# A decode kernel whose instruction orders are written out: rearranged from token 1's first dense chain on

## The chip, the cores and the metric

The kernel runs on one core of one Trainium2 chip. Its time is that of one execution on the device, in microseconds (us). TensorE is called PE (its weight loads PEld), VectorE DVE, ScalarE ACT, GpSimd POOL, and SyncE SP; SP issues the loads.

## The reference

Four tokens, one position each, go twice through the same pair of layers: attention over a cache (the last 2048 of 8192 positions, 16 query heads on 8 key/value heads of width 256), then a gated feed-forward layer. Each is added to its input.

```python
W = min(4096, max(256, Sk // 4))                       # 2048
q = (x @ wq).reshape(B, Sq, Hq, Dh).transpose(0, 2, 1, 3)      # B 4, Sq 1, Hq 16, Dh 256
k = jnp.repeat(k_cache[:, :, Sk - W:, :], rep, axis=1)
v = jnp.repeat(v_cache[:, :, Sk - W:, :], rep, axis=1)
p = softmax(jnp.einsum("bhqd,bhkd->bhqk", q, k) * Dh ** -0.5)
o = jnp.einsum("bhqk,bhkd->bhqd", p, v)                # then transposed, reshaped, @ wo
...
g = silu(x @ w_gate); u = x @ w_up; return (g * u) @ w_down    # 448 -> 1792 -> 448
...
x = x + A(layernorm(x)); x = x + B(layernorm(x))
x = x + A(layernorm(x)); x = x + B(layernorm(x))
```

Both layers use the same weights and the same cache, so the keys and values that the second layer needs are those that the first has read, as far as they are still on the chip.

## The kernel before

A program on the host first builds a list of operations (`Graph.op`, L196; `Graph.dma`, L224), each with its engine and with what it reads and writes; from these follow the semaphore waits (`_place_waits`, L316). The order in which each engine runs its operations is not planned: it is written out as five lists of operation numbers, `SEQ_PE`, `SEQ_DVE`, `SEQ_ACT`, `SEQ_POOL` and `SEQ_SP`, near the top of the file. The number of an operation is its place in the order of building. `schedule` (L240) takes the lists as they stand. Each engine runs its list strictly in order, so an operation whose input is late holds up all behind it on its engine.

A `w` in `SEQ_PE` is a filler: one matmul of 512 columns by a weight of zeros into the bank A, which changes no result (L1253). `HELD` says, for each operation outside PE that touches bank A, behind how many fillers it comes.

K and V are loaded in halves of 512 KB into 31 slots and, once the query weights have been used for the last time, into the 7 places that these took (`SLOTS`; L976 and L978 for K, L992 for V). A load into a slot that is in use waits until the last PE operation that reads the old content is through; SP issues the loads in the order of `SEQ_SP`, and a load that waits holds up those behind it.

The unit of attention work is a group: two key/value heads of one token, or of two. `PLAN` says which. Its steps:

- L982: DVE transposes each half of K in place (four per group).
- L1023: POOL or DVE spreads the query (`qe`).
- L1016: PE, the scores, a block of 64 short matmuls or fewer (L1016 operations free K slots); L1031: DVE takes the maximum.
- L1036, L1039: PE spreads the maximum; L1045: DVE; L1049: ACT, the exponential.
- L1060: PE turns the probabilities; L1068: ACT copies; L1076, L1081: their sum; L1103: POOL, its reciprocal.
- L1090: PE, probabilities by V, in four parts (these free V slots); L1105, L1107, L1113, L1123: to the attention output.
- L1143 or L1135: PE, the output projection by `wo`, as a row or as a column.

When all groups of a token's layer are through, its dense chain follows, one token alone: the residual (L883 to L903), the norm (L589 to L629), gate and up (L801, 56 matmuls each in four operations, closed by L816), the activation (L832, L835), gate times up (L846), down (L853, four operations), the second norm, and the query projection of the next layer (L683 to L722). The first layer's chains of the tokens 1, 2 and 3 run near 125 to 145, 177 to 194 and 229 to 250 us of the profiled execution.

The numbers that the change moves and the prediction names:

| numbers | what | engine |
|---|---|---|
| 559 to 562, 564 to 567 | first chain: gate, up | PE |
| 572 to 575 | first chain: down | PE |
| 655, 660 | scores and turn of the probabilities of a group of token 0's second layer | PE |
| 627 to 630 | probabilities by V of a group of token 2 | PE |
| 888 to 891, 893 to 896 | second chain: gate, up | PE |
| 901 to 904 | second chain: down | PE |
| 947 | scores of token 3's first group | PE |
| 934, 936, 940, 942 | transposes of that group's K halves | DVE |
| 878 to 880 | second chain: the norm's sums | DVE |
| 1211, 1215, 1217 | transposes of K halves of token 1's second layer | DVE |
| 1091, 1126 | maxima of two groups of token 3 | DVE |
| 1163 to 1166, 1168 to 1171 | third chain: gate, up | PE |
| 1176 to 1179 | third chain: down | PE |
| 1174, 1175 | third chain: L835, L846 | DVE |
| 1231 to 1234 | probabilities by V of a group of token 1's second layer | PE |
| 1269, 1263, 1265 and 1276 | transposes and scores of a group of token 2's second layer | DVE, PE |

Of the kernel before, what the change touches and what calls it, by code (L numbers as in the profile page):

```python
# [62 lines left out]
    "49 w w w w w 53 w w w 56 w 64 w w w w 67 w 75 w 78 w 86 w 99 89 w 100 102 103 105 w w w 106 w 108 w w w w w 134 "  # L63
    "171 136 173 w w 139 204 141 176 w w 206 143 144 209 178 145 146 180 w 211 w w w w w w 213 214 215 216 150 245 "
    "155 156 247 w w 181 182 183 250 w w 252 187 254 255 256 257 220 w w 227 228 229 230 261 268 270 271 w w 275 w "
    "278 284 288 289 290 285 291 286 287 343 w w w 345 297 298 299 348 300 w 350 w 304 352 315 316 308 317 353 319 "
    "320 322 w w w 323 325 354 355 w 368 391 370 359 w w 393 362 363 373 414 396 375 398 400 401 402 377 378 403 379 "
    "380 416 384 419 w w 421 w w 407 w w w w w w w w w 387 388 423 424 425 426 w 410 411 w w w 451 453 w w w w w 486 "
    "456 430 w w 488 433 434 458 460 461 491 462 w 493 495 496 w w w w w w 521 463 497 498 523 467 w w 526 w w 528 "
    "470 w 502 618 471 530 505 620 506 531 532 533 623 542 w 625 w 537 544 545 w w w 559 560 561 548 627 628 552 562 "  # L70
    "w w w w w 564 565 566 567 655 563 568 657 w 572 573 574 660 575 w 662 w 579 590 591 583 592 664 594 595 597 629 "
    "630 598 w w 665 666 600 634 w w 637 638 697 720 699 w 722 741 667 702 w 743 w 704 w 671 725 706 707 708 727 709 "
    "746 674 675 729 748 730 731 732 750 751 752 678 713 753 w w w w 780 682 736 w w w 782 757 716 717 w 785 w 815 "
    "686 760 761 787 762 763 817 789 790 791 w 820 w 822 792 824 825 w w w 796 w w w w w 850 799 800 852 855 826 827 "
    "857 w w w 859 860 831 w w 834 835 861 862 871 866 w w w w w w 873 874 877 888 889 881 890 891 w w w 893 894 895 "
    "896 947 892 897 w 949 w 901 902 903 904 952 w 908 w 919 954 920 912 956 921 923 924 957 926 958 959 927 929 w "
    "963 w w 966 967 993 972 995 w w w w w 974 1018 977 w w w 998 979 w w 1000 1020 981 982 983 984 1002 1003 1004 "
    "1005 988 w w w w w w w 1009 w w 1023 w w 1053 1025 1012 1013 1014 1015 1055 w w w 1027 1028 1058 1029 1030 1060 "
    "w w w w w 1062 w 1034 w w 1125 w 1090 1127 w w w w 1092 1063 1222 1064 1095 w 1224 w 1097 1065 1130 1099 1100 "
    "1101 1069 1102 1132 1074 1075 1227 1072 1134 1106 1073 1229 w 1109 1110 1135 1136 1137 1146 w w w w 1141 w w "  # L80
    "1148 1149 1152 1163 1164 1156 1231 1165 1168 1169 1166 1167 1232 1233 1170 1171 1172 w w w w w w 1276 1176 1177 "
    "1278 1178 1179 w 1281 1183 1194 1234 1283 1187 1195 1198 1196 1199 1238 1285 1286 1201 1202 1241 1242 1287 1204 "
    "1299 1341 1245 1301 w w w w w 1304 1368 1343 1288 1306 1249 w 1370 1253 1308 1309 1292 1310 1311 1346 1403 1348 "
    "1315 1373 w 1405 1320 1318 1319 1321 1350 1351 1352 1353 1408 1375 1324 1377 1378 1410 1357 1328 1379 1380 1412 "
    "1413 1414 1415 1332 1362 1384 1364 1365 1387 1419 1388 1422 1423 1426 1441 1442 1430 1443 1444 1446 1447 1445 "
    "1448 1449 1450 w w w 1456 1457 1458 1459 w w 1461 w w w"
).split()
# [1242 lines left out]
```

## Time and profile before

| | |
|---|---|
| median of 3 runs | 279.63 us (278.82 to 279.69) |
| profiled execution | 279.5 us |
| its span | 277.7 us |
| mean granted clock of PE | 0.97 |
| PE busy | 209.0 us (75%) |
| DVE busy | 173.8 us (63%) |
| loads, mean over the span | 346 GB/s read |
| fillers (L1253) | 223 |

The span runs from the first to the last instruction of the program. Busy shares are means over stages with different limits, so the windows of single stages say more. PEclk is the share of PE's clock that was granted. "DMA" is the busy share of the core's DMA engines; at 1.00 and above, the stream of loads is full. A line with "issue" in the chain is time in which the engine waited for nothing that the profile shows. SPq is SP's queue, in which the loads are issued.

### The profile page before, as it was taken

Reading aid. Unit: us, or ns where it says so; the run is one execution under the profiler, and the core shown is the slowest. Engines: PE = TensorE matmul, PEld = TensorE weight load, DVE = VectorE, ACT = ScalarE, POOL = GpSimd, SP = SyncE. Lnnn points to the kernel's source line nnn. Section 1 sums busy time; section 2 is a strip of 40 time slices with the busy share of each in tenths; the row PEclk is TensorE's granted clock in tenths of the full one; section 3 lists DMA queues with packets and bytes.
Section 4 is the critical chain, followed back from the end, with each engine's and each line's share of the span. In section 5 each row is a group of like instructions: output and inputs, shape, how many; then the busy total and the mean of one; then the engine's idle time right before and its main releaser. Section 6 shows DMA issues by size and latency. Waiting matters only on the chain.

```text
span 277.7 us, 9966 instructions
## 1 busy us (share of the span) xinstructions
PE 209.0 (75%) x4424; PEld 125.0 (45%) x4424; DVE 173.8 (63%) x522; ACT 47.3 (17%) x115; POOL 76.5 (28%) x195
## 2 busy tenths in 40 slices
PE   0000076699788968988998897899699798899997
PEld 0000032355464634455754444474454356456694
DVE  7973056445545799368447995655789845559751
ACT  0000000232111220121113221211022031032510
POOL 1000017142204412421253342124132332043650
PEclk9999999999989999999999999999979999599998
DMA  7999999999999999999799999939999999589200
GB/s 292 394 419 412 403 412 406 402 396 401 389 379 405 357 396 415 407 409 353 260 332 410 409 405 411 405 150 362 362 417 407 410 408 346 215 279 408 79 5 1
DMA packets 28474, 96.68 MB, mean 348 GB/s; under 512 B 2828, under 2 KB 6928, under 8 KB 27792
## 3 DMA queue, kind: packets, MB, share of 16 engines
q1 hardware_dynamic: 28423, 96.06, 88.8%
q8 instruction: 34, 0.56, 0.8%
q14 instruction: 9, 0.07, 0.1%
q10 hardware_dynamic: 8, 0.00, 0.0%
HBM read 96.05 MB, written 0.00 MB: 346 GB/s over the span
## 4 chain that ended last, share of the span: by engine, by line
PE 43%; DMA 25%; DVE 13%; SPq 10%; issue 4%; ACT 3%; POOL 2%; ACTq 0%
DMA half<-in_A_k_cache_dram 16%; PE A L1253 10%; DMA half<-in_A_v_cache_dram 9%; PE S L1016 8%; DVE half L982 7%; PE Y L1090 6%; SPq L992 5%; PE Z L801 4%; SPq L976 3%; PE Z L683 3%; SPq L558 2%; PE Z L853 2%; PE A L1143 2%; PE Y L1060 2%; PE A L1135 2%
## 5 line engine op out<-in xcount | busy, mean ns | idle before, releaser
L982 DVE STREAM_TRANSPOSE half<-half 128x1024 uint32<-128x1024 uint32 x80 | 97.2, 1231 | 22.3 <-DMA half<-in_A_k_cache_dram 22.2
L1253 PE MATMUL A<-identb,small 128*128 128x512 bf16 x223 | 67.4, 404 | 0.3 <-DVE xr L903 0.3
L1103 POOL TENSOR_TENSOR small<-small 128x4 f32<-128x4 f32 x32 | 32.5, 1017 | 70.1 <-DVE small L1081 64.7
L1090 PE MATMUL Y<-half,pT 128*8 128x256 bf16 x1024 | 38.7, 275 | 3.2 <-issue 1.4
L1016 PE MATMUL S<-half,qe 128*8 128x256 bf16 (+1 forms) x1120 | 35.3, 269 | 6.3 <-issue 2.0
L1016 PEld LDWEIGHTS S<-half,qe 128*8 128x8 bf16 x1120 | 24.4, 84 | 16.2 <-issue 3.8
L1023 POOL TENSOR_TENSOR qe<-qc,small 128x64 bf16<-128x64 bf16 x56 | 15.3, 295 | 47.6 <-PE S L1016 33.9
L921 PE MATMUL Z<-identb,wo_sb 4*128 4x4 bf16 x4 | 0.3, 167 | 36.7 <-DMA wo_sb<-in_A_x_dram 36.7
L1031 DVE TENSOR_REDUCE small<-S 104x1 bf16<-104x256 f32 x32 | 13.4, 417 | 22.0 <-PE S L1016 22.0
L1090 PEld LDWEIGHTS Y<-half,pT 128*8 128x8 bf16 x1024 | 21.3, 85 | 12.0 <-DVE small L1081 3.2
L1253 PEld LDWEIGHTS A<-identb,small 128*128 128x128 bf16 x223 | 19.1, 103 | 14.9 <-issue 6.4
L1105 ACT ACTIVATE oh<-Y 128x256 bf16<-128x256 f32 x32 | 12.2, 383 | 36.2 <-PE Y L1090 27.2
L615 POOL TENSOR_SCALAR st<-st 128x1 f32<-128x1 f32 x16 | 4.5, 280 | 50.1 <-DVE st L609 50.1
L1107 DVE SCALAR_TENSOR_TENSOR oh<-oh,small,Y 128x256 bf16<-128x256 bf16 x32 | 15.0, 469 | 4.0 <-ACT oh L1105 3.8
L921 PEld LDWEIGHTS Z<-identb,wo_sb 4*128 4x128 bf16 x4 | 0.2, 104 | 36.6 <-DMA wo_sb<-in_A_x_dram 36.6
L1143 PE MATMUL A<-wo_sb,oT 128*4 128x448 bf16 x200 | 13.8, 352 | 1.3 <-DVE oT L1123 1.3
L1049 ACT ACTIVATE praw<-S,small 104x256 bf16<-104x256 f32 x16 | 7.6, 472 | 38.9 <-DVE small L1045 38.9
L1049 ACT ACTIVATE praw<-S,small,st 104x256 bf16<-104x256 f32 x16 | 9.0, 564 | 30.1 <-DVE small L1045 26.6
L1068 ACT ACTIVATE pT<-Y 128x192 bf16<-128x192 f32 x32 | 10.5, 329 | 15.5 <-PE Y L1060 14.1
L683 PE MATMUL Z<-half,small 128*5 128x512 bf16 x160 | 10.9, 379 | 1.5 <-DVE small L592 1.4
L1081 DVE TENSOR_REDUCE small<-Y 128x4 f32<-128x64 f32 x32 | 6.7, 213 | 7.8 <-PE Y L1076 7.6
L1060 PE MATMUL Y<-selt,praw 104*64 104x48 bf16 x256 | 10.1, 197 | 1.8 <-ACT praw L1049 1.7
(135 smaller groups left out, 245.8 us busy)
## 6 DMA issues: line engine op xcount, KB each, us to landing
half<-in_A_v_cache_dram SPq DMA_DIRECT2D x80, 512.0 KB, 13.5
half<-in_A_k_cache_dram SPq DMA_DIRECT2D x76, 512.0 KB, 10.7
wo_sb<-in_A_wo_dram SPq DMA_DIRECT2D x8, 448.0 KB, 11.8
half<-in_A_wq_dram SPq DMA_DIRECT2D x3, 1024.0 KB, 16.2
half<-in_A_k_cache_dram SPq DMA_DIRECT2D x2, 1024.0 KB, 6.4
wd_sb<-in_B_w_down_dram SPq DMA_DIRECT2D x1, 1568.0 KB, 18.5
wu_sb<-in_B_w_up_dram SPq DMA_DIRECT2D x1, 1344.0 KB, 11.8
wg_sb<-in_B_w_gate_dram SPq DMA_DIRECT2D x1, 1344.0 KB, 14.7
```

The source lines that it names most:

```text
L683: last = e.matmul(zb[32 * j:32 * j + B + 1, 0:512], lhsT=lhsT, rhs=wq_sb[:, c:c + 512], start=(cc == 0), stop=(cc == 3), skip_group_check= ...
L982: return e.transpose(a, a)
L992: g.dma(pp + VLAG, 1 << 19, lambda e, cell=cell, hv=hv, vsrc=vsrc: e.dma_start(unit(cell), vsrc[hv]), None, w=(f"v{t}_{kvh}_{hv}",), run=4 ...
L1016: last = e.matmul(Sb[s_][qd:qd + 8, c0:c0 + rhs.free_size()], lhsT=qe[q_][:, P, ce, :, :].rearrange("p a n -> p (a n)"), rhs=rhs, start=(c ...
L1023: g.op(*((DVE, 0.13) if layer and fresh.get(t, gi) == gi else (POOL, 0.25)), pos - SLEAD - 1, lambda e, P=P, t=t, kvh=kvh: e.tensor_tensor ...
L1049: return e.activation(praw[0:R, 0:128 * n].rearrange("p (g r l) -> p g r l", g=2 * n, l=2), Sb[s_][0:R, 0:128 * n].rearrange("p (l g r) -> ...
L1060: last = e.matmul(Yb[p_][64 * h:64 * h + 64, c0:c0 + (48 if n == 2 else 32)], lhsT=praw[0:R, 64 * gg:64 * gg + 64], rhs=w, start=(gg == 0) ...
L1090: last = e.matmul(Yb[p_][32 * gg:32 * gg + M, 256:512], lhsT=pT[pt][:, gg, 2 * a + hv, 4 * P:4 * P + M] if n == 2 else p1[:, gg % 2, 2 * a ...
L1103: g.op(POOL, 0.69, pos, lambda e: e.tensor_tensor(ri[p_][:, 0:2 * n], rs[p_][:, 0:2 * n], expo[:, 1:1 + 2 * n], op=ALU.pow), r=(f"rs{p_}", ...
L1107: g.op(DVE, 0.43, pos, lambda e: e.scalar_tensor_tensor(out=oh[:, :], in0=oh[:, :], scalar=lomask[:, 0:1], in1=Yb[p_][:, 256:512], op0=ALU ...
L1143: last = e.matmul(Ab[32 * k:32 * k + B, 0:D], lhsT=oT[oi][:, k % 2, k // 2, :], rhs=wo_sb[:, 4 * kvh + k, :], start=False, stop=False, ski ...
L1253: return e.matmul(Ab[:, 0:512], lhsT=zero[:, 0:1].broadcast_to([128, 128]), rhs=identb[:, :].unsqueeze(1).broadcast_to([128, 4, 128]), sta ...
```

## The change

The five lists are written anew; the lists of SP and of the slots hold the same numbers in the same order as before (their lines are only broken differently). PE's list is the same up to 545 and the three fillers behind it (near 129 us of the profiled execution), DVE's, ACT's and POOL's are the same to about the same point. Behind it the operations stand in another order, and the fillers are placed anew: there are 188 in place of 223. The 99 fillers up to there are the same in both. `HELD` follows the new count of fillers. No operation other than fillers is added or taken away.

The lines of PE's list that hold the three chains (the old ones first):

```diff
-    "470 w 502 618 471 530 505 620 506 531 532 533 623 542 w 625 w 537 544 545 w w w 559 560 561 548 627 628 552 562 "
-    "w w w w w 564 565 566 567 655 563 568 657 w 572 573 574 660 575 w 662 w 579 590 591 583 592 664 594 595 597 629 "
-    "630 598 w w 665 666 600 634 w w 637 638 697 720 699 w 722 741 667 702 w 743 w 704 w 671 725 706 707 708 727 709 "
...
-    "857 w w w 859 860 831 w w 834 835 861 862 871 866 w w w w w w 873 874 877 888 889 881 890 891 w w w 893 894 895 "
-    "896 947 892 897 w 949 w 901 902 903 904 952 w 908 w 919 954 920 912 956 921 923 924 957 926 958 959 927 929 w "
...
-    "1101 1069 1102 1132 1074 1075 1227 1072 1134 1106 1073 1229 w 1109 1110 1135 1136 1137 1146 w w w w 1141 w w "
-    "1148 1149 1152 1163 1164 1156 1231 1165 1168 1169 1166 1167 1232 1233 1170 1171 1172 w w w w w w 1276 1176 1177 "
-    "1278 1178 1179 w 1281 1183 1194 1234 1283 1187 1195 1198 1196 1199 1238 1285 1286 1201 1202 1241 1242 1287 1204 "
...
-    "1448 1449 1450 w w w 1456 1457 1458 1459 w w 1461 w w w"
+    "533 623 542 w 625 w 537 544 545 w w w 548 559 560 552 627 561 562 628 w w w 655 564 657 563 565 566 567 568 660 572 "
+    "573 574 662 575 629 664 579 w 590 583 630 591 594 592 595 665 w 597 598 w 600 666 w w 697 720 699 634 w 722 667 702 "
...
+    "852 824 796 686 825 799 826 855 827 857 w 859 800 831 860 861 862 834 835 w w w 866 871 873 874 888 877 889 890 w 881 "
+    "891 w 947 892 893 894 895 896 897 949 901 902 903 904 952 w 954 908 919 920 912 921 956 923 924 926 957 w w 927 958 "
...
+    "1222 1072 1074 1075 1224 1134 1106 1073 1135 1109 1110 1227 1136 1137 1229 w 1141 1146 1148 1149 1152 1163 1164 1156 "
+    "1165 1166 1167 1168 1169 1170 1231 1171 1172 1232 w w w 1176 1177 1178 1179 1233 w w 1276 1183 1194 1195 1278 1187 "
...
+    "1423 1426 1441 1442 1430 1443 1444 1446 1445 1447 1448 1449 1450 w w 1456 1457 1458 1459 w 1461"
```

Of DVE's list, the lines around the second chain, the stretch behind it, and the third chain:

```diff
-    "758 837 816 687 692 788 818 839 843 823 795 845 798 797 851 853 858 830 832 833 870 865 934 872 867 868 936 875 "
-    "876 879 878 880 942 882 940 887 948 899 900 950 907 905 906 910 909 911 955 913 918 925 928 962 930 971 964 970 "
-    "965 1077 994 1042 996 973 975 1118 1048 1019 980 1120 1001 1040 987 1083 990 1008 1021 1046 1011 989 1010 1085 "
-    "1054 1209 1056 1026 1215 1217 1061 1033 1112 1114 1079 1035 1036 1126 1211 1128 1091 1093 1223 1225 1098 1068 "
-    "1070 1071 1133 1105 1107 1108 1230 1145 1147 1140 1142 1143 1150 1151 1154 1153 1155 1157 1162 1271 1174 1269 "
-    "1263 1265 1175 1277 1279 1180 1182 1181 1185 1184 1186 1284 1188 1237 1193 1200 1239 1240 1203 1205 1298 1297 "
-    "1398 1244 1300 1390 1302 1392 1246 1342 1247 1248 1251 1369 1252 1250 1307 1344 1291 1254 1396 1294 1259 1371 "
-    "1293 1314 1404 1317 1316 1349 1406 1323 1376 1356 1325 1326 1327 1411 1358 1330 1359 1329 1331 1361 1383 1333 "
...
+    "823 851 853 797 858 798 830 832 833 687 934 865 870 868 867 936 872 875 876 942 879 878 880 940 882 887 899 948 900 "
+    "950 905 906 907 910 911 955 909 913 918 925 928 930 962 1042 971 994 970 1077 973 975 964 1048 980 1120 996 1019 1040 "
+    "965 1046 1001 1021 1083 987 1085 1118 1026 1209 990 1054 1008 1056 989 1112 1010 1114 1079 1211 1091 1061 1126 1011 "
+    "1093 1033 692 1215 1098 1036 1035 1128 1217 1068 1071 1070 1105 1133 1223 1225 1107 1108 1145 1140 1142 1143 1147 "
+    "1150 1151 1154 1230 1153 1155 1157 1162 1271 1174 1269 1175 1263 1265 1180 1181 1185 1182 1186 1184 1277 1279 1188 "
+    "1193 1200 1237 1203 1240 1239 1205 1298 1297 1284 1398 1300 1244 1302 1390 1246 1392 1342 1247 1369 1344 1307 1291 "
+    "1396 1293 1248 1371 1294 1349 1314 1251 1404 1316 1317 1252 1406 1250 1376 1323 1356 1254 1325 1326 1411 1327 1330 "
+    "1331 1358 1359 1329 1361 1383 1385 1333 1418 1386 1259 1363 1420 1421 1424 1425 1428 1427 1338 1429 1431 1436 1451 "
```

More of the change, by code (lines that the diff above doesn't have):

```diff
@@ L62 @@
 SEQ_PE = (
[24 rows of a table removed]
[22 rows of a table added]
 ).split()
 SEQ_DVE = (
[18 rows of a table removed]
[18 rows of a table added]
 ).split()
 SEQ_ACT = (
[5 rows of a table removed]
[5 rows of a table added]
 ).split()
 SEQ_POOL = (
[8 rows of a table removed]
[7 rows of a table added]
 ).split()
 SEQ_SP = (
[7 rows of a table removed]
[7 rows of a table added]
 ).split()
 SLOTS = (
[4 rows of a table removed]
[4 rows of a table added]
 ).split()
 HELD = (
[L141 to L142 removed]
+    "0 44 44 44 94 94 99 99 120 122 123 123 130 133 133 133 178 178 179 179 184 184 185 185 185 185 185 185 185 185 185 "
+    "185"
 ).split()
```

2 lines of the change are left out of this document (removed), and 97 rows, old and new, of tables (SEQ_ACT, SEQ_DVE, SEQ_PE, SEQ_POOL).

## The prediction

> **What bounds the kernel now.** I read the page's slices and queues first, then the windows by stage, the issuing of the loads in the timeline, the chain, and last the granted clock.
>
> ```profile
> span 277.7 us, 9966 instructions
> PE 209.0 (75%) x4424; PEld 125.0 (45%) x4424; DVE 173.8 (63%) x522; ACT 47.3 (17%) x115; POOL 76.5 (28%) x195
> q1 hardware_dynamic: 28423, 96.06, 88.8%
> ...
> L1253 PE MATMUL A<-identb,small 128*128 128x512 bf16 x223 | 67.4, 404 | 0.3 <-DVE xr L903 0.3
> ```
> ```profile
> 130.00:140.00 10.00, 9.53 (x240) 6.94 (x240) 5.29 (x26) 1.25 (x4) 2.61 (x6) 1.00 0.76 270
> 180.00:190.00 10.00, 9.56 (x254) 7.06 (x250) 5.68 (x25) 1.07 (x3) 1.91 (x7) 1.00 0.55 215
> 210.00:220.00 10.00, 8.68 (x176) 4.34 (x172) 10.00 (x16) 1.19 (x3) 3.19 (x8) 1.00 1.03 409
> 240.00:250.00 10.00, 9.39 (x194) 5.20 (x192) 4.03 (x22) 2.42 (x5) 2.94 (x8) 0.89 0.73 258
> 260.00:277.70 17.70, 15.41 (x430) 11.90 (x428) 7.36 (x41) 3.38 (x9) 6.59 (x13) 0.90 0.01 3
> ```
> ```profile
> 167.66 18.74 SPq L992 DMA_DIRECT2D half<-in_A_v_cache_dram  x4
> 234.53 8.68 SPq L992 DMA_DIRECT2D half<-in_A_v_cache_dram  x4
> ```
>
> The second fence gives, per window, its length, the busy time of PE, PEld, DVE, ACT and POOL, then granted clock, DMA share and GB/s. The cache stream is full (share 1.03) except in three stretches, 130 to 140, 180 to 190 and 240 to 250, and nothing is loaded in the last 17.7 us. Those stretches are the first dense chains of tokens 1, 2 and 3. There SP stands still (18.74 us for four issues, 8.68 for four), because a load waits until PE has read the slot that it overwrites, while PE, 94 to 96% busy, is in the dense chain. So the bound alternates: the stream between the chains, PE's order inside them, PE alone at the end. The profiled execution took 279.5 us (span 277.7 and 1.8 around it), 0.1 below the median of 279.63.
>
> **The change part by part.** Everything ahead of the first chain, the loads' order and the slots stay. I follow the three chains; times are of the trace before, "earlier" is minus.
>
> *First chain.* Old order: gate, five fillers, four up matmul groups (564 to 567), scores 655, down (572 to 575) with the probabilities' turn 660 behind three of its four parts. New: three fillers, 655 ahead of the up groups, and 660 ahead of the whole down projection.
>
> ```profile
> 131.39 1.24 PE L1253 MATMUL A<-identb,small 128*128 128x512 bf16 x5
> 132.46 1.55 PE L801 MATMUL Z<-small,wu_sb 128*128 128x32 bf16 x56
> 133.95 1.08 PE L1016 MATMUL S<-half,qe 128*8 128x256 bf16 x32
> 135.92 1.22 PE L853 MATMUL Z<-wide,wd_sb 128*128 128x32 bf16 x42
> 137.07 0.31 PE L1060 MATMUL Y<-selt,praw 104*64 104x48 bf16 x8
> ```
>
> The scores lose four up groups ahead of them (1.4 us, the 1.55 less its overlap with the next) and two fillers (0.4), so by PE's work they are up to 1.8 earlier, and with them the loads that overwrite that K. But two PV groups' places and the wait for the norm on DVE lie in the same 3 us; I take half, 0.9. Down then waits for 660, which waits for the softmax of 655: 137.07 - 0.9 + 0.3 = 136.5 instead of 135.92. That is +0.6, and with PV group 630 moved between the q matmuls +0.8 for the chain's end, which the first scores of token 1's second layer and the loads behind them wait for. Bounds: -0.9 (the chain follows the scores) to +1.4 (all that the scores gained is put before the chain's end). I take +0.8.
>
> *Second chain.* Scores 947 come ahead of the four up groups (893 to 896), and of the nine fillers in and just ahead of the gate four go.
>
> ```profile
> 182.29 0.81 PE L1253 MATMUL A<-identb,small 128*128 128x512 bf16 x3
> 182.93 1.55 PE L801 MATMUL Z<-small,wu_sb 128*128 128x32 bf16 x56
> 184.41 1.12 PE L1016 MATMUL S<-half,qe 128*8 128x256 bf16 x32
> ```
> ```profile
> 181.09 1.24 DVE L982 STREAM_TRANSPOSE half<-half 128x1024 uint32<-128x1024 uint32 x1
> 182.29 1.23 DVE L982 STREAM_TRANSPOSE half<-half 128x1024 uint32<-128x1024 uint32 x1
> ```
>
> By PE's work 947 could move by over 2 us, but it needs the K transposes, which end at 182.29 + 1.23 = 183.52. It starts at 184.41, so at most 0.9 is to be had. The down projection waits for gate and up together, whose sum with 947 is the same; the chain's end does not move. Bounds -0.9 and 0 (the norm's three DVE steps now stand behind the first transpose, which may eat the gain). I take -0.9, as the queue is dry there and takes any earlier issue.
>
> *Between the chains.* DVE is busy 10.00 of 210 to 220. The new order puts the transpose of token 1's K half (1211) ahead of the score reductions 1091 and 1126, and the two K halves 1215 and 1217 behind these. In the old order 1211 began at 219.39, behind 1126; a reduction that stands behind a transpose whose load is late waits for the stream.
>
> ```profile
> 219.05 0.43 DVE L1031 TENSOR_REDUCE small<-S 104x1 bf16<-104x256 f32 x1
> 219.39 1.23 DVE L982 STREAM_TRANSPOSE half<-half 128x1024 uint32<-128x1024 uint32 x1
> ```
>
> Bounds: 0 (the half is there in time) and +2.5 (two transposes of 1.23 in front). I take +0.9, under one transpose, since the same DVE work is only permuted.
>
> *Third chain.* Old: six fillers, scores 1276, then down (1176 to 1179). New: up ends before PV group 1232, three fillers, down, two fillers, 1276. On DVE the gate-times-up product (L846) comes behind one of three transposes instead of all three.
>
> ```profile
> 238.82 2.56 PE A L1253 x6
> 241.38 1.44 PE S L1016 x29
> 242.83 0.80 PE Z L853 x28
> ```
> ```profile
> 236.47 3.49 DVE L982 STREAM_TRANSPOSE half<-half 128x1024 uint32<-128x1024 uint32 x3
> 239.88 0.13 DVE L846 TENSOR_TENSOR wide<-wide,Z 128x14 bf16<-128x14 f32 x1
> ```
>
> The product can run 2.3 earlier (two transposes), at 237.6; three fillers less save 1.3 and the scores' 1.44 leave the chain, so down starts at about 238.2 instead of 242.83, 4.6 earlier. Scores and fillers (1.44 and 0.8) then come inside the rest of the chain: about 3 earlier at its end. But 1276 itself still waits for the third transpose (236.47 + 3.49 = 239.96) and now for down: 240.5 against 241.38. The four loads behind it move by only 0.9, and these fix the last landings near 260. So the end gets 0.9 at least; from the rest of the 4.6, PE does earlier what it otherwise does behind the last landing. Bounds -0.9 and -4.6; I take -2.0, nearer to the landings' end, as the last scores need the last K.
>
> *End.* In the last projection eight fillers become three. The three behind the last output step cost nothing (the store covers them), two lie on the chain: -0.4 (0 to -1.0).
>
> *Granted clock.* 35 fillers go in all (the x223 of the first fence to 188, counted in the order). What that does is read from four stretches of 3.41 us; the second fence counts the fillers alone in the stretches ahead (busy of PE and PEld, clock, DMA).
>
> ```profile
> 180.83:184.24 3.41, 3.41 (x114) 3.05 (x111) 2.81 (x9) 0.00 (x0) 1.38 (x4) 1.00 0.49 192
> 197.90:201.31 3.41, 1.21 (x34) 0.69 (x33) 1.91 (x3) 0.56 (x1) 0.00 (x0) 1.00 0.95 380
> 201.31:204.72 3.41, 3.41 (x31) 1.50 (x27) 2.02 (x4) 1.11 (x3) 1.18 (x3) 0.50 1.03 423
> 232.03:235.44 3.41, 3.15 (x111) 2.83 (x108) 1.91 (x10) 0.00 (x0) 1.02 (x5) 1.00 0.81 321
> 235.44:238.85 3.41, 2.64 (x69) 1.74 (x66) 2.81 (x5) 0.27 (x1) 0.66 (x2) 0.50 0.62 181
> ```
> ```profile
> 129.63:133.04 3.41, 1.24 (x5) 0.41 (x5) 1.00 0.78 293
> 180.83:184.24 3.41, 0.81 (x3) 0.22 (x3) 1.00 0.49 192
> 232.03:235.44 3.41, 0.00 (x0) 0.00 (x0) 1.00 0.81 321
> ```
>
> Chains with five and three fillers kept the clock; the one with none had half of it in the next stretch, although PE was busy 3.15 of 3.41. In a half-clock stretch a filler takes 2.56/6 = 0.43 instead of 1.24/5 = 0.25, so one costs at most 3.41/2 = 1.7 us of PE; the dense groups hardly slow down, so about 1.0. The new first chain keeps three, the second two instead of three (and three instead of six just ahead), the third has none beside the gate as before. I take 2.5 more such stretches: +2.5. Bounds 0 and 3 x 1.7 = +5.1.
>
> The Trainium skill, "TensorE: Matmul & The Clock Gate", Part 1, puts the half clock down to an idle stretch of about 3.4 us. Read as idle time, that would leave the clock alone here and this term at 0. The rows agree on the length of a stretch and speak against idleness as the only cause.
>
> *PE without a visible cause.*
>
> ```profile
> 199.86 1.32 issue
> 236.36 0.77 issue
> ```
>
> Inside one block of matmuls PE twice stands still, waiting for nothing shown, where it ran dense. With 70 PE instructions fewer and the order denser, these fall elsewhere: -2.1 (both gone) to +2.1 (two more); I take +0.5.
>
> **Sum:** 0.8 - 0.9 + 0.9 - 2.0 - 0.4 + 2.5 + 0.5 = +1.4; 279.5 + 1.4 = 280.9, and 281.0 beside the median.
>
> **The rivals.** *The clock holds (faster).* If the fillers that are left suffice and at most one more stretch at half clock appears, the clock and stall terms fall away: 0.8 - 0.9 + 0.9 - 2.0 - 0.4 = -1.6, 278.0; with the third chain at 4.6, 275.4. I name 277.0. For it: 0.81 us of fillers kept the second chain at 1.00. Against it: 232.03 to 235.44 lost the clock at 92% busy. It decides when two stretches or fewer are added. The rule of the Trainium skill named above belongs to this rival.
>
> *It cancels (no change).* The last landings move by under 0.9 and the rest goes into waits that PE has anyway: 279.6. For it: the stream at 1.03 for most of the time. Against it: 17.7 us at the end without loads, which PE's order alone sets.
>
> *DVE waits for the stream (clearly slower).* The second transpose before the reductions is late by its whole bound, +2.5 instead of +0.9, with three stretches at full price, +5.1 instead of +2.5: 281.0 + 4.2 = 285.2. For it: DVE has no idle time in 210 to 220. Against it: the half in question is there when the old order reaches it.
>
> **How the numbers follow.** 0.3% of 279.63 is 0.84 us, about what tells a change from none. Forecast 0.40, DVE rival 0.13: slower 0.53. The clock holds: faster 0.34. It cancels: 0.13. The range of the forecast alone is 280.5 to 283.5; 276.0 to 285.0 leaves about 1 in 10 on each side.
>
> **What would show it.** Right: L1253 x188; down of the third chain near 238 to 239; the second chain's score block near 183.6, not earlier; two to three more stretches of 3.41 us at a clock of 0.50; DVE idle before L1031 at 215 to 222. Wrong: PEclk at 9 through both chains, or a last landing before 257, or the score block of the second chain at 182, which would mean that the K halves came earlier than the stream allows here.

## The result, and the profile after

| | before | changed |
|---|---|---|
| median of 15 executions each, one chip | 279.06 us (276.76 to 281.31) | 282.59 us (279.92 to 287.12) |
| profiled execution (span) | 279.5 (277.7) | 282.59 (280.8) |
| mean granted clock of the profiled execution | 0.97 | 0.94 |
| PE busy | 209.0 us | 210.4 us |
| fillers | 223 | 188 |

The changed kernel is slower by 1.1% (ratio 1.0107, 95% interval 1.0068 to 1.0146). All ratios here leave out executions more than 1.5% above the fastest of their kernel (four of the changed kernel's fifteen), so they are not always the quotient of the medians beside them. Lines of the changed kernel are 3 lower than those of the kernel before: the filler is L1250, scores are L1013, K transposes L979, gate and up L798, down L850.

From the page of the changed kernel: its span, PE's busy time, the fillers, and the slices of granted clock (one digit for a fortieth of the span); behind it the same slices of the kernel before:

```profile
span 280.8 us, 9890 instructions
PE 210.4 (75%) x4389; PEld 124.0 (44%) x4389; DVE 173.9 (62%) x522; ACT 47.6 (17%) x115; POOL 75.2 (27%) x195
L1250 PE MATMUL A<-identb,small 128*128 128x512 bf16 x188 | 58.8, 410 | 1.1 <-ACT wide L880 0.6
...
PEclk9999999899889999997797998979999998999797
```
```profile
PEclk9999999999989999999999999999979999599998
```

PE does 35 matmuls less and is busy for 1.4 us longer: what it does has become slower. The windows by stage of the changed kernel (columns as in the prediction):

```profile
130.00:140.00 10.00, 9.69 (x215) 6.44 (x219) 3.97 (x13) 1.09 (x3) 1.58 (x5) 0.66 0.68 232
180.00:190.00 10.00, 8.29 (x203) 5.74 (x194) 6.94 (x20) 1.20 (x3) 1.50 (x5) 0.83 0.25 94
240.00:250.00 10.00, 8.39 (x179) 4.94 (x179) 6.27 (x21) 1.77 (x4) 2.22 (x7) 1.00 0.76 261
260.00:280.80 20.80, 17.72 (x479) 13.38 (x472) 9.50 (x57) 4.52 (x11) 8.37 (x22) 0.83 0.05 19
```

The first chain ran at 0.66 of the clock where the old one had 1.00. In the second chain the loads moved 94 GB/s in place of 215. SP's queue shows that stretch directly: the four V loads up to the second chain's scores took 18.74 us from the first issue to the last, and now

```profile
168.64 21.35 SPq L989 DMA_DIRECT2D half<-in_A_v_cache_dram  x4
```

Where the time went, by the starts of the same operations and the landings of the same loads in the two profiled executions (changed minus before, us):

| place | PE | loads |
|---|---|---|
| ahead of the first chain (545; load landing at 127.9) | -0.4 | -0.6 |
| end of its down projection (575) | +2.0 | |
| loads landing at 155 to 175 | | -0.1 to -0.3 |
| last output projection ahead of the second chain (835) | +4.2 | -0.6 (at 184.5) |
| scores in the second chain (947) | +3.0 | +4.4 (behind it, at 197) |
| ahead of the third chain (1163; load 1212) | +2.7 | +5.0 |
| down of the third chain (1176) | -0.4 | |
| last landing; end of the span | +3.1 | +2.5 |

Up to 175 us the stream of loads had lost nothing: it absorbed the late first chain. Then PE came 4.2 us late to the second chain. The next load waits for the scores of that chain (947 ended at 188.85, the load was issued at 188.89), so the stream ran dry for longer, and from there on everything was late by what the stream had lost.

**Why PE came late to the second chain.** For each operation of PE I took the time from the end of the one ahead of it, or from its own start if that is later, to its end (a stop inside an operation counts as its time); the same operations in both traces.

| stretch of the changed kernel | real operations, now and before | fillers | idle |
|---|---|---|---|
| first chain, 127.5 to 140.9 (before 127.9 to 138.7) | 10.10, 8.08 | 2.30 (7), 2.43 (11) | 1.04, 0.73 |
| 140.9 to 181.0 (before 138.7 to 176.5) | 28.38, 25.62 | 7.83 (27), 7.78 (32) | 3.41, 4.06 |

Fillers and idle time hardly changed; the same real work takes 4.8 us longer. 3.45 us of that (1.81 and 1.64) lie in operations inside stretches at half clock, and 1.9 us in one score block, 815. Against that stands 1.0 us less in operation 730, in which the trace before has a stop (0.59 us, at 154 us). These are the stretches of 3.41 us of the changed kernel, the cold ones (at half clock) from 127 us on and two that precede one (PE, PEld, DVE, ACT, POOL, clock, DMA share, GB/s):

```profile
130.14:133.55 3.41, 3.32 (x49) 1.82 (x49) 2.37 (x5) 0.00 (x0) 0.77 (x3) 0.50 0.48 169
133.55:136.97 3.42, 3.37 (x62) 1.86 (x61) 0.68 (x3) 0.07 (x1) 0.65 (x2) 0.50 0.68 211
147.20:150.62 3.42, 1.48 (x57) 1.26 (x48) 2.21 (x6) 0.10 (x1) 1.00 (x4) 1.00 1.03 412
150.62:154.03 3.41, 3.36 (x52) 1.55 (x48) 1.82 (x3) 1.63 (x4) 0.00 (x0) 0.50 1.03 410
164.27:167.68 3.41, 1.69 (x52) 1.07 (x44) 1.41 (x7) 0.07 (x1) 0.47 (x2) 1.00 1.02 406
167.68:171.09 3.41, 3.41 (x37) 1.37 (x37) 2.83 (x9) 0.76 (x2) 1.05 (x2) 0.50 1.03 407
184.75:188.16 3.41, 3.41 (x74) 2.37 (x74) 2.73 (x9) 0.00 (x0) 0.64 (x3) 0.50 0.00 0
235.95:239.36 3.41, 3.41 (x110) 3.09 (x106) 2.32 (x11) 0.27 (x1) 1.76 (x7) 0.50 0.93 363
259.84:263.25 3.41, 3.41 (x64) 1.93 (x56) 1.98 (x14) 0.96 (x3) 1.44 (x5) 0.50 0.30 120
273.50:276.91 3.41, 3.41 (x100) 2.77 (x97) 0.89 (x4) 0.25 (x1) 1.37 (x4) 0.50 0.02 5
```

Eight, and a part of a ninth at the very end, against four in the kernel before from 127 us on. The two stretches with clock 1.00 are half empty (PE busy 1.48 and 1.69 of 3.41), and half clock follows each. PE's own rows around them:

```profile
134.06 1.88 PE L1013 MATMUL S<-half,qe 128*8 128x256 bf16 x32
...
150.01 0.19 PE L1033 MATMUL S<-small,identb 104*104 104x32 bf16 x1 [1.95 <-DVE small L1028]
...
164.12 0.76 PE L1013 MATMUL S<-half,qe 128*8 128x256 bf16 x28
166.50 0.63 PE L1013 MATMUL S<-half,qe 128*8 128x128 bf16 x20 [1.62 <-issue]
...
241.28 0.19 PE L813 MATMUL Z<-wide,identb 128*128 128x14 bf16 x1 [1.31 <-issue]
...
242.39 1.55 PE L850 MATMUL Z<-wide,wd_sb 128*128 128x32 bf16 x56
```

Block 655 took 1.88 us at half clock where it had taken 1.08. Block 815, at 164.12, stood still in its middle for 1.62 us, waiting for nothing that the profile shows; without that stop PE would have been busy for 3.3 of the 3.41 us ahead of the cold stretch at 167.68.

### The profile page after: what moved, and what is told of

It is laid out like the page before. It is cut to its first block, busy times and chain, and to the rows that moved or that the text cites. A ratio compares the mean times of both kernels' runs of the same rounds, so it can differ in the third digit from the quotient of the medians.

```text
span 280.8 us, 9890 instructions
## 1 busy us (share of the span) xinstructions
PE 210.4 (75%) x4389; PEld 124.0 (44%) x4389; DVE 173.9 (62%) x522; ACT 47.6 (17%) x115; POOL 75.2 (27%) x195
## 4 chain that ended last, share of the span: by engine, by line
PE 48%; DMA 18%; DVE 14%; SPq 10%; issue 4%; ACT 3%; POOL 2%; ACTq 0%
DMA half<-in_A_k_cache_dram 15%; PE Y L1087 9%; PE S L1013 8%; PE A L1250 8%; DVE half L979 8%; PE Z L798 5%; SPq L989 5%; DMA half<-in_A_v_cache_dram 3%; PE Z L850 3%; SPq L973 3%; PE A L1140 3%; PE Y L1057 2%; SPq L555 2%; PE Z L680 2%; PE A L1132 2%
## 5 line engine op out<-in xcount | busy, mean ns | idle before, releaser
L979 DVE STREAM_TRANSPOSE half<-half 128x1024 uint32<-128x1024 uint32 x80 | 97.5, 1232 | 27.2 <-DMA half<-in_A_k_cache_dram 27.0
L1250 PE MATMUL A<-identb,small 128*128 128x512 bf16 x188 | 58.8, 410 | 1.1 <-ACT wide L880 0.6
L1087 PE MATMUL Y<-half,pT 128*8 128x256 bf16 x1024 | 41.5, 280 | 4.0 <-DVE small L1078 2.1
L1013 PE MATMUL S<-half,qe 128*8 128x256 bf16 (+1 forms) x1120 | 37.9, 280 | 5.3 <-issue 2.3
L1013 PEld LDWEIGHTS S<-half,qe 128*8 128x8 bf16 x1120 | 24.9, 87 | 16.8 <-issue 4.0
L1087 PEld LDWEIGHTS Y<-half,pT 128*8 128x8 bf16 x1024 | 20.3, 85 | 11.6 <-DVE small L1078 4.1
L1250 PEld LDWEIGHTS A<-identb,small 128*128 128x128 bf16 x188 | 16.0, 104 | 17.0 <-issue 8.6
L1140 PE MATMUL A<-wo_sb,oT 128*4 128x448 bf16 x200 | 14.7, 352 | 1.4 <-DVE oT L1120 1.3
L680 PE MATMUL Z<-half,small 128*5 128x512 bf16 x160 | 11.8, 409 | 1.5 <-DVE small L589 1.3
L1120 DVE TENSOR_TENSOR oT<-Y,small 128x4 bf16<-128x4 f32 x64 | 8.3, 157 | 5.6 <-PE Y L1110 3.0
```

The source lines that it names most:

```text
L680: last = e.matmul(zb[32 * j:32 * j + B + 1, 0:512], lhsT=lhsT, rhs=wq_sb[:, c:c + 512], start=(cc == 0), stop=(cc == 3), skip_group_check= ...
L979: return e.transpose(a, a)
L1013: last = e.matmul(Sb[s_][qd:qd + 8, c0:c0 + rhs.free_size()], lhsT=qe[q_][:, P, ce, :, :].rearrange("p a n -> p (a n)"), rhs=rhs, start=(c ...
L1087: last = e.matmul(Yb[p_][32 * gg:32 * gg + M, 256:512], lhsT=pT[pt][:, gg, 2 * a + hv, 4 * P:4 * P + M] if n == 2 else p1[:, gg % 2, 2 * a ...
L1140: last = e.matmul(Ab[32 * k:32 * k + B, 0:D], lhsT=oT[oi][:, k % 2, k // 2, :], rhs=wo_sb[:, 4 * kvh + k, :], start=False, stop=False, ski ...
L1250: return e.matmul(Ab[:, 0:512], lhsT=zero[:, 0:1].broadcast_to([128, 128]), rhs=identb[:, :].unsqueeze(1).broadcast_to([128, 4, 128]), sta ...
```

## The experiments

The two orders can be joined at places where nearly the same operations have been issued in both: behind the first chain's down projection (138.6 us of the trace before, 140.9 of the changed one), behind the second chain's query projection (191.8, 196.6), ahead of the third chain (232.0, 234.8) and behind it (250.4, 252.4). Up to a join a kernel has the one order, behind it the operations that are left in the other; the orders of all four engines, the fillers and `HELD` go with it. So each part of the change can be made alone. The other runs move only fillers.

### Each part alone

First chain alone (PE's list; the other engines likewise):

```diff
-559 560 561 548 627 628 552 562 w w w w w 564 565 566 567 655 563 568 657 w 572 573 574 660 575 w 662 w 579
+548 559 560 552 627 561 562 628 w w w 655 564 657 563 565 566 567 568 660 572 573 574 662 575 629 664 579 w
```

> The changed order only for the first dense chain (up to its down projection, some 127 to 141 us); from there on the order before, 219 fillers. Theory 'dry spell' (the time is lost where the scores of the second chain, 947, come 3.0 us later and the loads behind them land 4.4 later; before that the stream had caught up, its loads landing 0.25 us earlier than before at 155 to 175): this part alone costs 0 to +0.5 us. Theory 'clock' (each stretch at half clock costs about 1 us wherever it lies; the first chain got two of them): +2 us, with 130 to 137 at half clock again.

Measured: 280.89 against 278.17, ratio 1.0105 (1.0073 to 1.0137), near +2.9 us. That is more than the clock theory said, and its profile (280.57 us) has cold stretches at 130 and 140 us, not from 130 to 137. The stream did not absorb this chain: its loads landed 0.9 early at 128 and 2.3 late at 169, where in the whole change they were 0.2 early. So the theory that a late first chain costs nothing falls for this part by itself.

Second part alone, from behind the first chain to the second chain's query projection (168 entries of PE's list; its first and last ones):

```diff
-591 583 592 664 594 595 597 629 630 598 w w 665 666 600 634 w w 637 638 697 720 699 w 722 741 667 702 w
+629 664 583 630 591 594 592 595 665 w 597 598 w 600 666 w w 697 720 699 634 w 722 667 702 741 704 w w
...
+954 908 919 920 912 921 956 923 924 926 957 w w 927 958 959
```

> The changed order only from behind the first chain to the second chain's query projection (some 139 to 197 us), the order before ahead of it and behind it, 213 fillers. Theory 'dry spell': this part alone carries +2.5 to +3.5 us, and the second chain's scores (947) start near 187. Theory 'clock': +1 to +2, for the stretches at half clock near 150, 168 and 185, and 947 near 185.5.

Measured: 283.24, ratio 1.0213 (1.0168 to 1.0258), the dearest part, above what either theory expected. Its profiled execution is the slowest of its six (286.89 us) and was 3.4 us late already at 128 us, in code that it shares with the kernel before; from there the stream lost 6 us more, all of them at the second chain (3.0 late ahead of it, 9.5 behind it). The stop in block 815 came again, in the same place:

```profile
168.90 0.65 PE L1016 MATMUL S<-half,qe 128*8 128x256 bf16 x24
171.30 0.66 PE L1016 MATMUL S<-half,qe 128*8 128x256 bf16 x24 [1.75 <-issue]
```

The stretch between the chains alone, and everything from the third chain on alone:

```diff
-958 959 927 929 w 963 w w 966 967 993 972 995 w w w w w 974 1018 977 w w w 998 979 w w 1000 1020 981 982
+927 958 959 929 w w w w 993 w w w w w 972 963 w 974 w w w 977 w 979 1018 995 966 981 982 1020 983 984
```
```diff
-1231 1165 1168 1169 1166 1167 1232 1233 1170 1171 1172 w w w w w w 1276 1176 1177 1278 1178 1179 w 1281
+1165 1166 1167 1168 1169 1170 1231 1171 1172 1232 w w w 1176 1177 1178 1179 1233 w w 1276 1183 1194 1195
...
-1448 1449 1450 w w w 1456 1457 1458 1459 w w 1461 w w w
+1448 1449 1450 w w 1456 1457 1458 1459 w 1461
```

> The changed order only from behind the second chain to ahead of the third (some 192 to 235 us), 215 fillers. In the trace of the changed kernel PE came 4.0 us late into this part and 2.7 late out of it. Theory 'dry spell': -1 to 0 us, since the stream, not PE's order, sets the times here. Theory 'DVE waits for the stream', a rival of the prediction: +1 to +2.5.

> The changed order only from the third chain on, 210 fillers. In the trace of the changed kernel the third chain's down projection went from 2.7 us late ahead of the chain to 0.4 early, and the last landing and the end were again 2.5 and 3.1 late. Theory 'the third chain gains what it gained there': -1 to -2.5 us. Theory 'the last landings decide' (the loads near 243 to 248 wait for the scores and PV groups, which move little): -0.5 to +0.5.

Measured: the stretch between, 278.51, ratio 0.9998 (0.9965 to 1.0031): nothing. From the third chain on, 282.60, ratio 1.0120 (1.0074 to 1.0165). The gain that was forecast for the third chain isn't there. But this kernel's profile was 4 to 5 us late already ahead of 235 us, in code that it shares with the kernel before, so it was run once more, with the third chain alone beside it (the first two lines of the last diff, without the end).

> The changed order from the third chain on, as before in the runs, once more. In its first profile everything up to 235 us, whose instructions are those of the kernel before, was 4 to 5 us late, from two stretches at half clock at 50 us on, and from 235 us to the end it won 1.4 us back. Theory 'the clock's grid' (the loss of 3.3 us was where the 3.41 us grid of the clock happened to lie over the first 60 us, and changes from one execution to the next): PE's 1200th matmul at 115 to 118 us, in either case the stretch from 235 us to the end 0 to 1.4 us shorter than before, and a median within 1 us of the kernel before. Theory 'the part itself costs': first 200 us on time and the end 2 to 3 us late.

> The changed order for the third chain alone (some 232 to 251 us), the order before ahead of it and for the end, 221 fillers. The prediction's term for it was -2.0 (-0.9 to -4.6). Theory 'the third chain gains by itself': -0.9 to -2. Theory 'it gains only where all comes late' (the down projection moves, but the loads behind the chain wait for PV group 1231, which stands later in the new order): -0.5 to +1.

Measured: from the third chain on, 281.94, ratio 1.0043 (1.0003 to 1.0082); the third chain alone, 280.55, ratio 1.0071 (1.0036 to 1.0106). The two runs of the one kernel differ by 0.8%, with intervals that barely overlap, so part of the first 1.2% was probably not the order; the sign is the same three times. The forecast of a median within 1 us was missed: the eleven executions of the second run lie between 277.56 and 285.46 us. That identical code up to 235 us differs from execution to execution shows in the profiles: in the windows 48 to 58 and 58 to 235 of the kernel before, of the first run and of the second, the same instructions got

```profile
48.00:58.00 10.00, 7.57 (x135) 4.00 (x139) 4.60 (x11) 2.75 (x5) 2.62 (x10) 1.00 1.03 400
58.00:235.00 177.00, 154.12 (x3323) 91.45 (x3314) 117.22 (x319) 35.34 (x90) 52.07 (x122) 0.98 0.97 378
```
```profile
48.00:58.00 10.00, 7.87 (x89) 3.12 (x93) 3.91 (x10) 1.97 (x2) 1.97 (x7) 0.66 1.01 392
58.00:235.00 177.00, 153.81 (x3271) 90.66 (x3264) 116.10 (x311) 36.25 (x91) 52.44 (x122) 0.97 0.96 368
```
```profile
48.00:58.00 10.00, 8.11 (x97) 3.32 (x101) 3.84 (x8) 1.97 (x2) 1.89 (x8) 0.66 1.00 388
58.00:235.00 177.00, 154.72 (x3355) 92.03 (x3344) 117.36 (x322) 36.20 (x91) 52.39 (x122) 0.99 0.97 376
```

a clock of 1.00 or of 0.66 around 50 us, 135 or 89 to 97 matmuls in the ten, and 3323, 3271 or 3355 in the 177 behind. The clock near 50 us is the same in the two runs, so it is not what parts them: the first had two more cold stretches, at 132 and 153 us, the second none up to 235, and PE came to the third chain (1163) 3.7 us late in the first and 0.5 us in the second.

What the new third chain costs shows in SP's queue. In the kernel before, the four V loads begin 11.15 us behind the four K loads ahead of them (223.38 and 234.53). With the new third chain alone they begin 14.59 behind:

```profile
225.52 1.75 SPq L976 DMA_DIRECT2D half<-in_A_k_cache_dram  x4
240.11 5.14 SPq L992 DMA_DIRECT2D half<-in_A_v_cache_dram  x4
```

They wait for PV group 1231, which stood behind the gate (ahead of 1165) and stands behind almost all of up now. In the whole change the wait is 9.42 us, against 7.49 with the old third chain behind the same first three parts. I take it that the down projection's head start is paid there; no run moves 1231 alone.

### Parts together

The first two parts, and the first three (everything up to the third chain):

> The changed order from the first chain up to the second chain's query projection, the order before behind it, 209 fillers. The first part alone cost 2.9 us and the second alone 5.9. If the parts add up: +8 to +9. Theory 'joints' (each part is arranged for what comes ahead of it, and the loss of a part alone is largely the joint between an old and a new order): +2.5 to +4.5, no more than the whole change and one joint.

> The changed order up to the third chain, the order before from there on, 201 fillers. The whole change cost 3.0 us, and its first two parts alone 5.3. Theory 'the third chain gains in its place' (in the changed kernel's trace the loads' lateness fell from 5.0 us ahead of it to 2.5 behind it): +4.5 to +6. Theory 'the rest makes up for it': +3.0, as the changed kernel.

Measured: two parts 285.05 against 279.57, ratio 1.0189 (1.0116 to 1.0262); three parts 281.63 against 278.93, ratio 1.0063 (1.0026 to 1.0100). The sum of the first two alone would be 1.0318, so they don't add up. The part between the chains, which is worth nothing in the old order, wins back about 1.2% behind the new first two (their intervals don't meet). And without its third chain and its end the change costs no more than with them (1.0063 against 1.0107, intervals that overlap). The kernel with three parts, old third chain, has its block 815 stop too:

```profile
163.81 0.76 PE L1016 MATMUL S<-half,qe 128*8 128x256 bf16 x28
166.20 0.63 PE L1016 MATMUL S<-half,qe 128*8 128x128 bf16 x20 [1.64 <-issue]
```

### Fillers and clock

Weak fillers in the order before:

```diff
-                return e.matmul(Ab[:, 0:512], lhsT=zero[:, 0:1].broadcast_to([128, 128]),
+                return e.matmul(Ab[0:32, 0:512], lhsT=zero[:, 0:1].broadcast_to([128, 32]),
```

> The kernel before, with all 223 fillers as long as they were (512 columns) but on 32 of the array's 128 columns, so that PE is busy just as long and a quarter of the array works. Theory 'the clock goes by how much of the array works': many more stretches of 3.41 us at half clock (mean granted clock below 0.90), and by the prediction's price of about 1.0 us each, with five to ten more, +5 to +10 us. Theory 'the clock goes by idle time alone': clock 0.97 and 0 us.

Measured: 281.88 against 279.57, ratio 1.0123 (1.0064 to 1.0182). The filler's row (line and tile, nanoseconds, first and last start, form) shows the same length, on a quarter of the columns; behind it the granted clock in the page's slices:

```profile
L1253 PE MATMUL A<-identb,small x223: 376/379/634, 36.7 to 277.9; 128*32 128x512 bf16 x112
```
```profile
PEclk9999999999899999997999999979979999799977
```

(375/378/654 ns minimum, median and maximum in the kernel before.) It is +3.4 us in place of +5 to +10, and the clock is not what costs it. The profiled execution has six cold stretches from 127 us on in place of four and a mean clock of 0.957, but over the four executions the clock was 0.957, 0.976, 0.976 and 0.957, and in the eleven of the kernel before beside them 0.951 to 0.981, with the same mean of 0.967. At 0.957 the weak fillers took 282.51 and 282.90 us, the kernel before 279.57 to 280.12; at 0.976 they took 280.76 and 281.25, the kernel before at 0.975 took 276.64 and 278.36. So the theory by which the clock goes by how much of the array works falls, as far as four executions can tell, and what the weak fillers cost instead is open.

The fillers of the one kernel in the order of the other, operation by operation (the first entries of PE's list that differ):

```diff
-552 562 w w w w w 564 565 566 567 655 563 568 657 w 572 573 574 660 575 w 662 w 579
+w w w 552 562 564 565 566 567 655 563 568 657 572 573 574 660 575 662 579 w
```
```diff
-628 w w w 655 564 657 563 565 566 567 568 660 572
+w w w w w 628 655 564 657 w 563 565 566 567 568 660 572
```

The first of these has the order before and 188 fillers, the second the changed order and 223.

> The order before, but each operation of PE is followed by as many fillers as in the changed kernel, 188 in all: the change's fillers without its order. Theory 'clock' (the forecast's term of +2.5 comes from the 35 fillers): +1.5 to +3.5 us and three or more additional stretches at half clock. Theory 'order' (the fillers do nothing for the time, the order of the real work makes the 3 us): -0.8 to +0.8.

> The changed order, but each operation of PE is followed by as many fillers as in the kernel before, 223 in all: the change's order without its fillers. Theory 'clock': the loss of 3 us shrinks to 0 to +1.5 us over the kernel before, with at most six stretches at half clock. Theory 'order': +2.5 to +4, as the changed kernel or worse by the PE time of 35 fillers.

Measured: 286.37, ratio 1.0291 (1.0238 to 1.0343), and 296.28, ratio 1.0605 (1.0536 to 1.0675). Both theories fall. Neither the number of fillers nor the order of the real work explains these, since the first has the old order and the second the old number. More fillers did not hold the clock either: it was 0.919 to 0.936 in the six executions of the second, and 0.926 to 0.957 in the changed kernel. My reading, which no run isolates, is that a filler put where another order had a wait holds up the operation behind it, up to eight of them at one place.

Last, 23 fillers more in the changed kernel, only where its trace shows PE idle:

```diff
-697 720 699 634 w 722
+697 720 w w w w w w 699 634 w 722
...
-1304 1368 w 1288
+1304 1368 w w w w w 1288
```

> The changed kernel with 23 more fillers, put only where its own trace shows PE idle between 129 and 257 us (six behind 720, where it stood 1.95 us, ahead of the stretch at half clock at 150.6; the rest in ten gaps of 0.3 to 1.3), 211 in all. Theory 'clock' (in the changed kernel's trace the real matmuls up to the second chain take 3.45 us longer in the stretches at half clock from 130 to 171): the stretch near 150 goes, one or two others with it, and 1 to 2 us come back, so the loss against the kernel before falls from 3.0 to 1 to 2. Theory 'strict order' (a filler that isn't placed for just this order holds up what comes behind it, as in the runs with exchanged fillers): no gain or slower than the changed kernel, +3 to +6.

Measured: 284.81 against 279.34, ratio 1.0203 (1.0148 to 1.0257). In its profile the two cold stretches at 150.6 and 167.7 are gone, and the score block behind the new fillers takes 1.08 us in place of 1.88.

```profile
150.40:153.82 3.42, 3.20 (x64) 1.88 (x62) 1.57 (x5) 1.72 (x4) 0.00 (x0) 1.00 1.00 335
...
167.47:170.88 3.41, 3.38 (x47) 1.40 (x47) 3.41 (x13) 1.66 (x4) 0.98 (x2) 1.00 1.03 407
```
```profile
149.17 1.47 PE L1253 MATMUL A<-identb,small 128*128 128x512 bf16 x6
...
151.82 1.08 PE L1016 MATMUL S<-half,qe 128*8 128x256 bf16 x32
```

But the six executions took 282.39 to 289.19 us, and the profiled one is the fastest of them. With the clock held in two places the kernel is not faster, rather slower. But the clock as a whole was hardly higher: cold stretches came at 140 and, one more than before, at 236 and 270 us, and the mean clock of the six executions is 0.944, that of the changed kernel's fifteen 0.940. So the run does not decide whether the lost clock is what costs the 3 us in most executions. That is shown for the one profiled execution, by its own rows.

## Why the prediction was right, and where it was not

The forecast was 281.0 us and slower; measured are 282.59, and +3.1 us between the two profiled executions where the sum said +1.4. The range held it. That it came out so near is partly luck: two of the order's steps failed, and more clock was lost than the sum had. Of the signs that the prediction named, the 188 fillers came; the scores of the second chain began at 187.4 and not near 183.6, the down projection of the third at 242.4 and not near 238 to 239, and there were four more cold stretches, not two to three. The steps one by one:

- **First chain** (+0.8, -0.9 to +1.4). The down projection ends 2.0 us later, but 1.8 of that is half clock; 0.2 is left for the order. Its cost for the stream was nil in the whole change.
- **Second chain** (-0.9, -0.9 to 0). This step failed. "By PE's work 947 could move by over 2 us, but it needs the K transposes": it looked at the scores' place inside the chain and took for granted that PE would come to the chain as early as before. PE came 4.2 us late, DVE stood behind it with the residual (L882), and the transposes of the scores' K halves, whose loads had landed in time, came behind that; the last ended at 185.96 + 1.24 = 187.20, and 947 started at 187.44 instead of 183.6. The rows, first of the kernel before, then of the changed one:

```profile
176.41 0.54 ACT L883 ACTIVATE wide<-A 128x448 bf16<-128x448 f32 x1 [2.04 <-PE A L1143]
...
176.99 0.62 DVE L885 TENSOR_TENSOR wide<-A,wide 128x448 bf16<-128x448 f32 x1 [1.29 <-ACT wide L883]
```
```profile
180.81 0.54 ACT L880 ACTIVATE wide<-A 128x448 bf16<-128x448 f32 x1 [0.18 <-PE A L1140]
...
181.41 0.82 PE L1250 MATMUL A<-identb,small 128*128 128x512 bf16 x3 [0.64 <-ACT wide L880]
...
182.27 0.62 DVE L882 TENSOR_TENSOR wide<-A,wide 128x448 bf16<-128x448 f32 x1 [0.99 <-PE Y L1110]
...
182.95 1.23 DVE L979 STREAM_TRANSPOSE half<-half 128x1024 uint32<-128x1024 uint32 x1
...
185.96 1.24 DVE L979 STREAM_TRANSPOSE half<-half 128x1024 uint32<-128x1024 uint32 x1
```

Not all of that is lateness from ahead. In the new order three fillers stand between the two halves of the residual, ACT's and DVE's, and `HELD` has DVE's half wait for the third (the row names L1110, but the program's wait is for the filler). So it began 1.46 us behind the start of ACT's half in place of 0.58: 0.9 us, which comes back in all five profiles of this order with the fillers kept there. The prediction counted fillers that go and did not look at what those that stay hold up.

What stands in a chain is worth nothing until the lateness of its beginning has been added up.

- **Between the chains** (+0.9, 0 to +2.5). Alone it is 0. In the changed kernel DVE did wait 0.74 us for a load at 221 us, two transposes ahead of a score reduction (1091), since the loads were 5.0 us late; but its scores ended only at 223.44 and it began at 223.52, so the wait cost nothing there. The bound of two transposes in front is not in the lists: 1211 alone moves ahead of the reductions, and 1215 and 1217 move behind them.
- **Third chain** (-2.0, -0.9 to -4.6). This step failed too: alone the part is 0.7% slower, and nowhere in the runs did it gain over the old order. Two causes show. The V loads behind PV group 1231 begin 3.4 us later, counted from the K loads (1.9 in the whole change), a queue that the prediction didn't follow when it moved 1231. And the trace before was a bad sample there: its third chain had lain in two cold stretches and a stop (235.44 to 242.27, and 0.77 us at 236.36). In seven other profiles with the old third chain (first chain alone, second part alone, stretch between, two parts, three parts, both kernels of the old order with other fillers) the lateness of the loads, against the trace before, shrank from load 1212 to the last one by 1.5 to 3.9 us; in five with the new one by 0.8 to 2.5 (in the sixth, the changed order with 223 fillers, it grew by 2.5). What the changed kernel wins there, the old order wins as well whenever it comes late. I read an accident of one execution as a property of the order.
- **End** (-0.4). From the last landing to the end of the span it was 17.7 us and is 18.3; two cold stretches lie in it instead of one.
- **Granted clock** (+2.5 from 2.5 stretches of 1.0). Right in kind, too small in number. There are 4 more stretches and a part of a fifth; the four up to 171 us cost 3.45 us of real work, 0.86 each. Over the eleven executions of the changed kernel that its ratio counts, time falls with mean clock (0.931 to 0.957, correlation -0.71), 95 us for a clock of 1, so about 0.6 us for one stretch of 3.41 (3.41 x 0.5 / 281 x 95). The price of 1.0 was of the right size, rather high. That fillers are the way to change it was not: the runs with other fillers all lost.
- **Stops of PE** (+0.5, -2.1 to +2.1). Behind 127 us there were three stops over 0.5 us of 0.59, 1.32 and 0.77, and there are two, of 1.62 and 1.31: +0.25 in all. What counted was the place. One now lies inside block 815, ahead of the second chain, in the profiles of five of the six kernels with the new second part (1.33 to 1.75 us).

Clock (4.1 x 0.86 = 3.5) and stops (0.25) together come to more than the 3.1 that were lost. What is left for the order itself, about -0.6, with the 0.9 us at the residual in it, is a remainder and not a measurement; the order's own terms of the prediction were -1.6.

Of the rivals, "the clock holds" was wrong on its condition: more than two stretches were added. The page of the Trainium skill that goes with it, "TensorE: Matmul & The Clock Gate", Part 1, by which an idle window of about 3.4 us lowers the clock, would have seen none coming; here two stretches with PE busy for 1.48 and 1.69 of 3.41 us were followed by half clock, and so was, in the trace before, one with 3.15. "It cancels" did not come, and "DVE waits for the stream" only as a wait of 0.74 us that cost nothing.

What stays open is how much of the 3 us in the other fourteen executions is clock. An estimate from the record: the 59 executions of the kernel before that the other runs' ratios count had a mean clock of 0.971 and lost 98 us for a clock of 1 (correlation -0.79), the changed kernel's eleven had 0.943, and 0.028 x 98 is 2.7 us, nearly all of it. But time and clock going together does not say which causes which, and the weak fillers lost 1.2% at an unchanged clock. The parts made alone cost more when added up than the whole change does, so runs of parts can't be summed; and the run that held the clock in two places lost time elsewhere.

## What to carry to other kernels

An order that was arranged with the durations of one trace has that execution's clock and stops in it; before a stage's gain is counted, look whether the stage lay in a cold stretch or a stop in just that trace, and compare several executions of it. To see why a stage is late, set the occupied time of the same operations side by side, stage by stage, apart from fillers and idle time: here that split 4 us into half clock and one stop at once. And look at what each filler that stays is waited for by: three at the residual held DVE up by 0.9 us. Parts of such an order, and its fillers, belong together: the second part of the change alone cost 2.1%, and other fillers 2.0% to 6.1%, where the whole change cost 1.1%.

## What was unexpected of the hardware

- **The clock's grid makes identical code differ.** The granted clock changes at the ends of stretches of 3.41 us, and these lie differently over the program in each execution. In the profiles of the kernel before and of those that share its first 127 us, PE's 1200th matmul began at 115.0 to 115.9 us where no cold stretch or a single one lay at 48 to 51 us, and at 116.9 to 118.8 where two in a row began there (in one profile, a single one at 52.7). The kernel before alone took 276.6 to 282.5 us over the chips used; how much of that is the clock was not isolated.
- **PE stops at a fixed count of instructions.** Counted over all of PE's instructions in the trace (matmuls, weight loads and waits), every stop of over 0.35 us without a visible cause stands at the 194th or 195th of a block of 256: 1219, 4035, 5827 and 7106 in the kernel before, 1219, 4291 and 7107 in the changed one, and the same in the other profiles. Most of the block ends have none. The queue of instruction data (q8) moved 34 pieces of 16 KB in every kernel, and the traces tie the stops to them: each stop ends 1.26 to 1.63 us after the piece of the same number as the block has landed (in block 815, landed at 165.23, work goes on at 166.50), and in none of the fourteen traces does PE begin the 196th instruction of a block sooner than 1.2 us after its piece. So these are waits for code that comes late. Where such a stop falls inside work that PE is the bound of, it costs its 0.6 to 1.75 us, and 35 fillers more or fewer move it to another place in the program; no run shifts the code alone.
- **A filler on a quarter of the array's columns kept the clock** (mean 0.967 over four executions, as with whole fillers), and still the kernel was 1.2% slower.
